# Block 0 enters w1's products centred only, and the tokens' scale is multiplied onto their sums

## The chip, the cores and the metric

The kernel runs on one core of one Trainium2 chip. The metric is the device time of one execution in microseconds (us), here the median of three timed runs. "Before" is the kernel as it stood, "after" the changed one.

## The reference

```python
xn = _layernorm(x, axis=-1)            # (x - mean) / sqrt(var + 1e-5), over 640 columns
A  = Real(DFT_seq(DFT_hidden(xn)))     # four einsums with the cosine and sine matrices
B  = gelu(xn @ w1 + b1) @ w2 + b2      # tanh gelu; w1 is 640 x 1536, w2 is 1536 x 640
out = x + A + B                        # x is 1 x 2048 x 640, fp32
```

What matters for the change: every token's row is centred by its mean and multiplied by one number of its own, 1/sqrt(var + eps). That number can be multiplied into the row before the product with w1, or onto the 1536 sums of that token after it, because it is the same for all 640 columns of a row.

## The kernel before, in words

The 2048 tokens are four blocks of 512, a block is four chunks of 128 rows. All products are in pairs of fp32r numbers: a value is split into a high part (a copy rounded by ScalarE, `high`, line 186) and a low part (what is left, subtracted by VectorE, `low`, line 189), and each product is three matmuls (high x high, high x low, low x high). So every operand that TensorE uses costs ScalarE one pass and VectorE one pass first.

The kernel's first stage, about 90 us long, is the MLP of block 0. It works in units of 128 of the 1536 hidden columns. `hidden(g)` (line 320) is 15 matmuls that accumulate w1's product of unit g in one of the PSUM banks 5, 6, 7; ScalarE takes gelu of the bank (line 340), the result is split, and `output(g)` (lines 300 to 302) is 15 matmuls into banks 0 to 4. The order on TensorE is hidden(0), hidden(1), hidden(2), output(0), hidden(3), output(1), and so on: in turn i of the loop at line 1157 come hidden(i+2) and output(i). Each turn also prepares W1[i+3] (`prep_w1`) and W2[i+1] (`prep_w2`), that is: a split of a weight piece that SyncE has loaded.

Beside that run pieces of other work, which `background(i)`, `late(i)` and `normalize_a` put into the turns: the statistics of the other blocks' rows (`ln_stats`, BN_STATS on VectorE), their scale (`ln_scale`, a square root on ScalarE and five small VectorE operations), the normalizing itself (`ln_apply`, line 231), and two rearrangements: the normalized rows of blocks 2 ("b") and 1 ("a") are moved within the on-chip memory into tiles z_b and z_a by 16 DMAs each (`put_z`, line 762; z_a lies in the tile `row`), and all rows are written to a DRAM tensor xn (`put_rows`, line 770). From z_b and z_a "forms" are made for the next stage: `make_forms` transposes a piece (line 259) and splits it. In before, forms of b are made in turn 4, those of a from turn 6 on.

All orders are written out by hand: each engine carries out its own list strictly in the order of the program, and waits at the first instruction whose inputs are not there. The same holds for SyncE's and GpSimd's lists of DMA issues.

The start. Four chunks of x are loaded; 19 matmuls on zeros (line 666) keep TensorE busy until then, and the first two weight loads wait for the first 7 and 10 of these (`NGATE`). The chunks' statistics are taken on VectorE (0, 2, 3: lines 215, 216) and on ScalarE (1: lines 692 to 699), the roots on ScalarE (690, 707) and polished by small VectorE operations (700 to 713), then the rows are normalized (714, 721 on ScalarE, line 236 on VectorE), 20 TensorE transposes turn them (line 682), and their results are split into XT (lines 186 and 189 under line 736). W1[0] is split at lines 723 and 734.

Of the kernel before, what the change touches and what calls it, by code (L numbers as in the profile page):

```python
# [10 lines left out]
F32 = mybir.dt.float32  # L11
F32R = mybir.dt.float32r
AF = mybir.ActivationFunctionType
# [6 lines left out]
NWARM = 19  # L20
# [6 lines left out]
def kernel(  # L27
# [105 lines left out]
    ident = early.tile([P, P], F32, name="ident")  # L133
    es_r = ExitStack()
# [41 lines left out]
    def split(hi, lo, src, perm=False):  # L176
# [6 lines left out]
        low(l, s, h)  # L183
# [26 lines left out]
    def ln_stats(c):  # L210
        m = MV
# [6 lines left out]
    def ln_scale(n):  # L218

        m = MV[:, :n]  # L220
        ve, r, t = m[:, :, 2], m[:, :, 3], m[:, :, 4]
# [7 lines left out]
    def ln_apply(c, eng=nc.vector):  # L229
        m = MV[:, slot[c]]  # L230
        eng.tensor_scalar(xt[c], xt[c], m[:, 0:1], m[:, 3:4], op0=ALU.subtract, op1=ALU.mult)

    def ln_apply_chunked(dst, c, j0=0, j1=ND):

        m = MV[:, slot[c]]
# [51 lines left out]
    def prep_w1(i, n=None):  # L287
        if i < NF:
            W1[i] = slots[1, i]
            split(W1[i][:, 0], W1[i][:, 1], w1r.pop(i if n is None else n).rearrange("p a b -> p (a b)"))  # L290

    def prep_w2(i):
        if i < NF:
            W2[i] = slots[2, i]
            split(W2[i][:, 0], W2[i][:, 1], w2r.pop(i), perm=True)
# [36 lines left out]
    def unit(g, acc, plus=None, a=None):  # L332
# [18 lines left out]
    FIRST = [(0, 0), (0, 2), (1, 0), (1, 2), (0, 1), (2, 0), (2, 2), (1, 1), (3, 0), (3, 2)]  # L351
    FIRST += [(2, 1), (4, 0), (4, 2), (3, 1), (4, 1)]
# [327 lines left out]
    def transpose_x(c, j0, j1):  # L680
# [5 lines left out]
    last = 1  # L686
    f, m = MV[:, 0], MV[:, last]
    root, step, shift = f[:, 3:4], f[:, 4:5], f[:, 5:6]
    ln_stats(0)
    nc.scalar.activation(root, f[:, 1:2], AF.Sqrt, bias=eps[:, 0:1])  # L690
    scratch = mr.tile([P, 2 * TB], F32, tag="hs", bufs=3, name="scratch")[:, :D]
    nc.scalar.activation(scratch, xt[last], AF.Copy, scale=-1.0 / D, accum_out=m[:, 5:6])
    nc.scalar.activation(
        chunked(xp[:, last]),
        xt[last].rearrange("p (q c i) -> p q c i", q=Q, i=B),
        AF.Identity,
        bias=m[:, 5:6],
    )
    nc.scalar.activation(scratch, xp[:, last], AF.Square, scale=D**-0.5, accum_out=m[:, 1:2])
    nc.vector.reciprocal(root, root)  # L700
    nc.vector.scalar_tensor_tensor(step, root, -0.5, root, op0=ALU.mult, op1=ALU.mult)
    nc.vector.scalar_tensor_tensor(step, f[:, 1:2], EPS, step, op0=ALU.add, op1=ALU.mult)
    for c in (2, 3):
        ln_stats(c)
    others = MV[:, 1:NC]
    v, r, t = others[:, :, 1], others[:, :, 3], others[:, :, 4]
    nc.scalar.activation(r, v, AF.Sqrt, bias=eps[:, 0:1])  # L707
    nc.vector.scalar_tensor_tensor(root, step, 1.5, root, op0=ALU.add, op1=ALU.mult)  # L708
    nc.vector.scalar_tensor_tensor(shift, f[:, 0:1], -1.0, root, op0=ALU.mult, op1=ALU.mult)
    nc.vector.reciprocal(r, r)  # L710
    nc.vector.scalar_tensor_tensor(t, r, -0.5, r, op0=ALU.mult, op1=ALU.mult)
    nc.vector.scalar_tensor_tensor(t, v, EPS, t, op0=ALU.add, op1=ALU.mult)
    nc.vector.scalar_tensor_tensor(r, t, 1.5, r, op0=ALU.add, op1=ALU.mult)
    nc.scalar.activation(  # L714
        chunked(xp[:, 0]),
        xt[0].rearrange("p (q c i) -> p q c i", q=Q, i=B),
        AF.Identity,
# [1039 lines left out]
```

## Time and profile before

| what | value |
|---|---|
| timed runs | 851.46, 851.7 and 852.76 us, median 851.7 |
| span of the profiled execution | 849.9 us, first to last instruction |
| what lies around the span | 1.8 us, taken as the median less the span; the profiled execution's own time is not listed apart |
| TensorE / weight loads / VectorE / ScalarE / GpSimd busy | 99% / 82% / 81% / 43% / 8% |
| granted TensorE clock, mean | 0.998 |
| DMA | 166.53 MB, 196 GB/s mean |

How to read what follows. "Idle before" an instruction is the time its engine had nothing to do, with what ended that time. The chain that ended last is followed back from the end of the kernel: whatever is not on it could have been longer without costing anything, up to its slack. A row with xN stands for N instructions in a row; its duration is from the start of the first to the end of the last, so the pitch of one is about a N-th of it.

### The profile page before, as it was taken

Reading aid. Unit: us, or ns where it says so; the run is one execution under the profiler, and the core shown is the slowest. Engines: PE = TensorE matmul, PEld = TensorE weight load, DVE = VectorE, ACT = ScalarE, POOL = GpSimd, SP = SyncE. Lnnn points to the kernel's source line nnn. Section 1 sums busy time; section 2 is a strip of 40 time slices with the busy share of each in tenths; the row PEclk is TensorE's granted clock in tenths of the full one; section 3 lists DMA queues with packets and bytes.
Section 4 is the critical chain, followed back from the end, with each engine's and each line's share of the span. In section 5 each row is a group of like instructions: output and inputs, shape, how many; then the busy total and the mean of one; then the engine's idle time right before and its main releaser. Section 6 shows DMA issues by size and latency. Waiting matters only on the chain.

```text
span 849.9 us, 10599 instructions
## 1 busy us (share of the span) xinstructions
PE 841.9 (99%) x3711; PEld 696.7 (82%) x3711; DVE 686.7 (81%) x909; ACT 368.6 (43%) x527; POOL 67.7 (8%) x116
## 2 busy tenths in 40 slices
PE   8999999999999999999999999999999999999997
PEld 7888888888888888888888888888888888888886
DVE  7979889767844778979978887889967998885687
ACT  7655666654453555443444344232323433323241
POOL 0440024222301000000000000000000000000002
PEclk9999999999999999999999999999999999999999
DMA  8995667878977897958744679763745799705464
GB/s 230 288 248 158 139 163 250 260 223 305 262 192 199 333 323 138 209 120 193 158 137 107 167 220 283 165 144 99 214 150 156 229 237 234 303 19 180 124 172 108
DMA packets 199141, 166.53 MB, mean 196 GB/s; under 512 B 61648, under 2 KB 170192, under 8 KB 198576
## 3 DMA queue, kind: packets, MB, share of 16 engines
q1 hardware_dynamic: 188320, 140.42, 62.7%
q0 software_dynamic: 7600, 24.91, 8.7%
q10 hardware_dynamic: 3168, 0.52, 0.3%
q8 instruction: 29, 0.48, 0.2%
q14 instruction: 24, 0.20, 0.1%
HBM read 115.75 MB, written 46.14 MB: 190 GB/s over the span
## 4 chain that ended last, share of the span: by engine, by line
PE 98%; DMA 1%; DVE 0%; ACT 0%; SPq 0%; issue 0%; ACTq 0%
PE banks L301 29%; PE banks L302 29%; PE banks L300 29%; PE banks L320 10%; DMA row<-in_A_x_dram 1%; PE banks L682 0%; DVE st L215 0%; ACT xp L714 0%; SPq L208 0%; DVE yo L1722 0%; DVE mv L216 0%; ACT mv L707 0%; DVE mv L708 0%; ACTq L707 0%
## 5 line engine op out<-in xcount | busy, mean ns | idle before, releaser
L186 ACT ACTIVATE as<-r 128x1024 fp32r<-128x1024 f32 x80 | 85.0, 1062 | 171.1 <-PE banks L302 150.4
L300 PE MATMUL banks<-as,xab 128*128 128x512 f32 x407 | 158.3, 389 | 0.0
L302 PE MATMUL banks<-as,xab 128*128 128x512 f32 x407 | 158.3, 389 | 0.0
L301 PE MATMUL banks<-as,xab 128*128 128x512 f32 x407 | 158.3, 389 | 0.0
L189 DVE TENSOR_TENSOR as<-r,as 128x1024 fp32r<-128x1024 f32 x80 | 97.2, 1215 | 38.1 <-ACT as L186 38.0
L301 PEld LDWEIGHTS banks<-as,xab 128*128 128x128 f32 x407 | 76.4, 188 | 15.9
L302 PEld LDWEIGHTS banks<-as,xab 128*128 128x128 f32 x407 | 76.4, 188 | 15.8
L300 PEld LDWEIGHTS banks<-as,xab 128*128 128x128 f32 x407 | 76.4, 188 | 15.8
L300 PE MATMUL banks<-as,xc 128*128 128x512 f32 x224 | 87.1, 389 | 0.0
L301 PE MATMUL banks<-as,xc 128*128 128x512 f32 x224 | 87.1, 389 | 0.0
L302 PE MATMUL banks<-as,xc 128*128 128x512 f32 x224 | 87.1, 389 | 0.0
L186 ACT ACTIVATE as<-rt 128x1024 fp32r<-128x1024 f32 x32 | 34.0, 1063 | 72.5 <-PE banks L302 57.9
L320 PE MATMUL banks<-xt,xab 128*128 128x512 f32 x240 | 56.8, 390 | 0.0
L189 DVE TENSOR_TENSOR hs<-ab,hs 128x512 fp32r<-128x512 f32 x36 | 24.7, 685 | 37.6 <-ACT hs L186 37.6
L320 PEld LDWEIGHTS banks<-xt,xab 128*128 128x128 f32 x240 | 45.0, 188 | 9.4
L301 PEld LDWEIGHTS banks<-as,xc 128*128 128x128 f32 x224 | 42.1, 188 | 8.8
L302 PEld LDWEIGHTS banks<-as,xc 128*128 128x128 f32 x224 | 42.0, 188 | 8.7
L300 PEld LDWEIGHTS banks<-as,xc 128*128 128x128 f32 x224 | 42.1, 188 | 8.7
L1280 POOL DMA_DIRECT2D out_dram<-u x4 | 2.6, 658 | 568.8 <-DVE u L463 568.8
L302 PE MATMUL banks<-hs,xc 128*128 128x512 f32 x120 | 46.7, 389 | 0.0
L300 PE MATMUL banks<-hs,xc 128*128 128x512 f32 x120 | 46.7, 389 | 0.0
L301 PE MATMUL banks<-hs,xc 128*128 128x512 f32 x120 | 46.7, 389 | 0.0
(240 smaller groups left out, 1678.9 us busy)
## 6 DMA issues: line engine op xcount, KB each, us to landing
raw<-in_A_dft_seq_re_dram SPq DMA_DIRECT2D x64, 256.0 KB, 5.4
raw<-in_A_dft_seq_im_dram SPq DMA_DIRECT2D x64, 256.0 KB, 5.1
w1r<-in_B_w_dram SPq DMA_DIRECT2D x144, 80.0 KB, 3.5
wit<-wst POOLq DMA_DIRECT2D x15, 384.0 KB, 4.2
wit<-wst POOLq DMA_DIRECT2D x20, 256.0 KB, 4.5
forms_ab<-xab SPq DMA_DIRECT2D x4, 1280.0 KB, 7.7
xab<-wit SPq DMA_DIRECT2D x13, 384.0 KB, 4.5
row<-xn SPq DMA_DIRECT2D x14, 320.0 KB, 5.3
```

The source lines that it names most:

```text
L186: nc.scalar.activation(h, s, AF.Copy)
L189: nc.vector.tensor_tensor(l, s, h.bitcast(F32), op=ALU.subtract)
L300: nc.tensor.matmul(acc, wh, mh, start=first, stop=False, skip_group_check=goes_on)
L301: nc.tensor.matmul(acc, wh, ml, start=False, stop=False, skip_group_check=goes_on)
L302: nc.tensor.matmul(acc, wl, mh, start=False, stop=last, skip_group_check=goes_on)
L320: nc.tensor.matmul(acc, W1[i][:, a, j * P : (j + 1) * P], XT[j][:, b], start=n == 0, stop=n == len(steps) - 1)
L1280: queues[q % len(queues)].dma_start(rows_of(out, t)[:, :, q * DQ + c0 : q * DQ + c1], src[q * B : (q + 1) * B])
```

## The change

- Chunks 0 to 3 are only centred before the transposes. Chunk 0 is centred by VectorE after its statistics, chunk 1 by ScalarE, chunk 2 by VectorE, chunk 3 by both; nothing waits for a root. The spread of chunk 3 and the four roots come after W1[1] is split.
- The scale (one number for each token) is turned by four TensorE transposes of a broadcast column, which stand after the first six matmuls of hidden(1), into bank 0; ScalarE copies it out. Each of the 12 units of block 0 gets a VectorE multiplication of its sums by this tile ahead of gelu.
- W1[0]'s high part moves from ScalarE to VectorE. 14 warm-up matmuls instead of 19.
- The normalizing of blocks 0 and 2 for z_b and xn moves from VectorE to ScalarE (`rows_beside`). Block 2's scale is made by a bit trick (two VectorE operations) and three Newton steps on GpSimd, 14 GpSimd operations in all with the shift; block 3's by the same steps on VectorE. Only block 1's scale keeps the square root of ScalarE.
- The low parts of W1[i+3] and W2[i+1] move behind the multiplication of unit i+2 on VectorE. From turn 4 on, the background comes after gelu(i+2).
- z_a's DMAs go out over GpSimd and SyncE in turn (before: GpSimd alone), xn's of block 2 over SyncE. Forms of a are made in turn 5 instead of 6, and so on.

```diff
-NWARM = 19
+NWARM = 14
...
+    def ln_scale(n, eng=nc.vector):
...
+        nc.vector.tensor_scalar(ve, m[:, :, 1], EPS, None, op0=ALU.add)
+        nc.vector.tensor_scalar(r.bitcast(I32), ve.bitcast(I32), -0.5, float(0x5F3759DF), op0=ALU.mult, op1=ALU.add)
+        for _ in range(3):
+            eng.tensor_tensor(t, r, r, op=ALU.mult)
+            eng.tensor_tensor(t, t, ve, op=ALU.mult)
+            eng.tensor_scalar(t, t, -0.5, 1.5, op0=ALU.mult, op1=ALU.add)
+            eng.tensor_tensor(r, r, t, op=ALU.mult)
...
+    def ln_apply_beside(c):
+        m = (MVA if 4 <= c < 8 else MV)[:, slot[c]]
+        nc.scalar.activation(xt[c], xt[c], AF.Identity, bias=m[:, 5:6], scale=m[:, 3:4])
...
+        if g < NF:
+            add(a, acc, scale, ALU.mult)
+            acc = a
         nc.scalar.activation(a, acc, AF.Gelu_apprx_tanh, bias=b1c[:, i : i + 1])
...
+    ln_stats(0)
+    centre(0)
+    mean_beside(1)
+    centre_beside(1)
+    spread_beside(1)
+    ln_stats(2)
+    centre(2, 0, 2)
+    mean_beside(3)
+    nc.vector.tensor_scalar(MV[:, 3, 0:1], MV[:, 3, 5:6], -1.0, None, op0=ALU.mult)
+    centre_beside(3, 0, 2)
+    centre(2, 2, ND)
+    centre(3, 2, ND)
     transpose_x(0, 0, ND)
+    transpose_x(1, 0, ND)
     transpose_x(2, 0, 2)
     transpose_x(3, 0, 2)
     transpose_x(2, 2, ND)
+    transpose_x(3, 2, ND)
+    W1[0], first_w1 = slots[1, 0], w1r.pop(0).rearrange("p a b -> p (a b)")
+    nc.vector.tensor_copy(W1[0][:, 0], first_w1)
     nc.vector.tensor_tensor(W1[0][:, 1], first_w1, W1[0][:, 0].bitcast(F32), op=ALU.subtract)
...
-    acc0 = hidden(0, slice(1, None))
+    acc0 = hidden(0)
     prep_w1(1)
-    acc1 = hidden(1)
+    spread_beside(3)
+    v, r, t = MV[:, :, 1], MV[:, :, 3], MV[:, :, 4]
+    nc.scalar.activation(r, v, AF.Sqrt, bias=eps[:, 0:1])
...
+    prep_w1(2)
     prep_w2(0)
-    prep_w1(2)
+    acc1 = hidden(1, slice(0, 6))
+    for c in range(NC):
+        nc.tensor.transpose(bank(0)[:, c * P : (c + 1) * P], MV[:, c, 3:4].to_broadcast([P, P]), ident)
+    hidden(1, slice(6, None))
+    scale = rows.tile([P, TB], F32, tag="yt", bufs=2, name="scale")
+    nc.scalar.activation(scale, bank(0), AF.Copy)
...
+    def rows_beside(i):
...
+        if i == 2:
+            Z["b"] = zo_tile("z_b")
+            for c in range(2 * NC, 3 * NC):
+                ln_apply_beside(c)
+            put_z(Z["b"], A["rows_b"], nc.gpsimd, nc.sync)
+            put_rows(2, A["rows_b"], nc.sync)
...
         if i == 1:
             ln_stats(11)
+            ln_scale(NC, nc.gpsimd)
+            ln_shift(nc.gpsimd)
...
-        if i == 6:
+        if i == 5:
             put_rows(1, A["rows_a"], nc.sync)
             new_forms(3, "t1")
             make_forms("a", "ua0", "ua1", "va0")
...
+        if i == 5:
+            add(ub, ub, ua, ALU.subtract)
...
-        put_z(Z["a"], A["rows_a"], nc.gpsimd)
+        put_z(Z["a"], A["rows_a"], nc.gpsimd, nc.sync)
...
     for i in range(NF - 2):
-        prep_w1(i + 3)
-        if i == 3:
-            normalize_a()
+        lows = []
+        prep_w1(i + 3, rest=lows)
...
-        prep_w2(i + 1)
+        prep_w2(i + 1, lows)
+        rows_beside(i)
+        if i < 4:
+            background(i)
+        acc = hidden(i + 2)
...
+        gelu(i + 2, acc, lambda k: [f() for f in lows] if k else None)
         if i + 6 < NF + 3:
             load_w1(i + 6)
         load_w2(i + 4)
-        background(i)
-        acc = hidden(i + 2)
...
-        gelu(i + 2, acc)
+        if i >= 4:
+            background(i)
         late(i)
         output(i)
```

In `gelu`, the function handed in as `fill` runs between the high and the low part of the unit, so `lows` (W1's and W2's low parts) stand on VectorE behind the unit's multiplication and ahead of its own low part. `late(3)` is now `normalize_a`. The loads of block 0's residual rows and of b2 move from turn 8 to turn 9.

More of the change, by code (lines that the diff above doesn't have):

```diff
@@ L182, in split @@
         high(h, s)
-        low(l, s, h)
+        if rest is None:
+            low(l, s, h)
+        else:
+            rest.append(lambda: low(l, s, h))
     def high(h, s):
@@ L699 @@
[L699 to L717, printed above, removed]
-        bias=shift,
-        scale=root,
-    )
@@ L1152, in fourier_step, with second @@
             form(2)
-    gelu(0, acc0)
-    gelu(1, acc1)
+    a0 = unit(0, acc0)
+    a1 = mr.tile([P, TB], F32, tag="ab", bufs=2, name="ab1")
+    def second(k):
+        if k:
+            add(a1, acc1, scale, ALU.mult)
+    split_unit(0, a0, second)
+    nc.scalar.activation(a1, a1, AF.Gelu_apprx_tanh, bias=b1c[:, 1:2])
+    split_unit(1, a1)
     for i in range(NF - 2):
-        prep_w1(i + 3)
-        if i == 3:
-            normalize_a()
+        lows = []
+        prep_w1(i + 3, rest=lows)
         if i == NF - 3:
```

120 lines of the change are left out of this document (65 added, 55 removed).

## The prediction

> **What bounds the kernel now.** First the page's busy times and its chain that ended last, then the same chain in order of time.
>
> ```profile
> PE 841.9 (99%) x3711; PEld 696.7 (82%) x3711; DVE 686.7 (81%) x909; ACT 368.6 (43%) x527; POOL 67.7 (8%) x116
> PE 98%; DMA 1%; DVE 0%; ACT 0%; SPq 0%; issue 0%; ACTq 0%
> 1.67 4.54 DMA row<-in_A_x_dram
> 6.23 0.90 DVE st L215 x2
> 7.36 0.76 DVE st L215 x2
> 8.66 0.91 ACT xp L714
> 9.71 2.27 PE banks L682 x19
> 25.79 3.40 PE banks L320 x15
> ```
>
> TensorE (PE) is the chain from 9.71 us to the end; ahead of it stand chunk 2's landing (1.67 + 4.54 = 6.21), the statistics and the normalizing. So a change can win only in the first 16 us, where TensorE waits for its operands, and it can lose wherever it makes TensorE wait later. A hidden(g) or an output(g) is 15 matmuls of 0.227, 3.40 us, and a turn 6.8.
>
> The second view is the timeline by engine, the start first.
>
> ```profile
> 0.75 1.82 SPq L208 DMA_DIRECT2D row<-in_A_x_dram  x4
> 1.44 1.10 DVE L657 CAST warm<-zeros 128x512 fp32r<-128x512 f32 x3
> 4.66 0.21 DVE L216 BATCH_NORM_AGGREGATE mv<-st 128x2 f32<-128x12 f32 x1
> 5.10 0.72 ACT L692 ACTIVATE scratch<-row 128x640 f32<-128x640 f32 x1
> 5.95 0.83 ACT L693 ACTIVATE xp<-row,mv 128x640 f32<-128x640 f32 x1
> 7.45 0.19 ACT L699 ACTIVATION_READ_ACCUMULATOR scratch<-xp 128x1 f32 x1
> 9.60 1.51 DVE L236 TENSOR_SCALAR xp<-row,mv 128x256 f32<-128x256 f32 x4
> 11.03 2.56 ACT L186 ACTIVATE xt<-banks 128x512 fp32r<-128x512 f32 x5
> 11.09 0.82 DVE L734 TENSOR_TENSOR xab<-w1r,xab 128x640 fp32r<-128x640 f32 x1
> 11.83 3.07 DVE L189 TENSOR_TENSOR xt<-banks,xt 128x512 fp32r<-128x512 f32 x5
> 22.23 0.39 PE L300 MATMUL banks<-hs,xc 128*128 128x512 f32 x1
> L666 PE MATMUL banks<-warm 128*128 128x512 f32 x12 | 5.4, 641 | 1.9 <-DVE warm L657 1.9
> DMA to landing us min/median/max: 3.0/4.0/4.9
> ```
>
> Output(0) starts at 22.23; hidden(1) and hidden(2) before it are 30 matmuls, so hidden(0) ended at 22.23 - 6.8 = 15.4. That is the mark to beat.
>
> **The start after the change.** x's four issues are some 0.46 apart from 0.75 on and land 3.0, 3.5 (twice the median less the third's), 4.54 (the chain's) and 4.9 later: 3.7, 4.7, 6.2, 7.0. ScalarE takes chunk 1 as in before (mean, centring, spread: from 5.10 to 7.64, 2.54 us), now from 4.7 on, to 7.2; then chunk 3's mean (0.9) to 8.1. VectorE negates it (some 0.2), centres the rest of chunks 2 and 3 (0.39 and 0.45 by the L236 row) to 9.1, copies W1[0] (1.10 / 3 for 512 columns, so 0.45 for 640) to 9.5, subtracts (0.74 to the next start) to 10.3, and takes five low parts of XT (0.60 each) to 13.3. The last matmul of hidden(0) waits for the fifth: hidden(0) ends at 13.65, **1.75 us sooner**. Were the copy as dear as the subtraction, it would be 1.4. TensorE hides none of this, and nothing else is late: 12 warm-up matmuls at 0.44 run to 7.2, two at 0.23 to 7.65, and the transposes follow the centred chunks to 9.8; ScalarE's five high parts (0.48 apart) run from 9.25 to 11.8.
>
> The four transposes of the scale cost TensorE 4 x 0.12 (2.27 / 19) = 0.48. Do they wait? Their place is six matmuls into hidden(1), at 15.0. The roots: ScalarE splits W1[1], takes chunk 3's spread and the root to 13.5; VectorE has W1[1]'s low part to 14.0 and four small operations (0.2 each) to 14.8. Cover 0.2; without it the transposes would wait by what is missing. So the start brings 1.75 - 0.48 = **-1.3** (between -0.9 and -1.8).
>
> **The turns.** Rows of the stage, those that set its waits:
>
> ```profile
> 1.06 0.29 POOL masks.py:199 TENSOR_SCALAR_AFFINE_SELECT ident<-ident 128x128 f32<-128x128 f32 x1
> 32.65 0.17 DVE L226 TENSOR_TENSOR mv<-mv 128x4 f32<-128x4 f32 x1
> 33.05 2.18 DVE L231 TENSOR_SCALAR r<-r,mv 128x640 f32<-128x640 f32 x4
> 33.91 0.74 ACT L186 ACTIVATE xab<-w1r 128x640 fp32r<-128x640 f32 x1 [1.72 <-DMA w1r<-in_B_w_dram]
> 35.90 4.36 POOL L762 DMA_DIRECT2D z_b<-r  x8 [8.54 <-ACT xc L186]
> 45.43 3.81 POOL L762 DMA_DIRECT2D row<-rt  x7 [2.76 <-DVE rt L231]
> 53.18 2.73 POOL L762 DMA_DIRECT2D row<-rt  x5 [1.13 <-DMA row<-rt]
> 58.38 0.69 DVE L189 TENSOR_TENSOR hs<-ab,hs 128x512 fp32r<-128x512 f32 x1 [0.42 <-ACT hs L186]
> 59.31 0.83 DVE L189 TENSOR_TENSOR as<-w1r,as 128x640 fp32r<-128x640 f32 x1 [0.24 <-ACT as L186]
> 62.69 1.30 DVE L259 STREAM_TRANSPOSE ztua<-row 128x512 f32<-128x512 f32 x2 [1.05 <-DMA row<-rt]
> 66.85 1.22 DVE L463 TENSOR_TENSOR z_b<-z_b,row 128x1024 f32<-128x1024 f32 x1
> 67.98 0.69 DVE L189 TENSOR_TENSOR hs<-ab,hs 128x512 fp32r<-128x512 f32 x1
> 66.43 2.88 PE L320 MATMUL banks<-xt,as 128*128 128x512 f32 x12
> 24.00:40.00 16.00, 16.00 (x72) 13.23 (x72) 14.99 (x38) 10.16 (x13) 6.43 (x12) 1.00 0.96 294
> 40.00:52.00 12.00, 12.00 (x55) 9.93 (x54) 9.69 (x22) 6.02 (x9) 8.39 (x16) 1.00 0.96 266
> 52.00:62.60 10.60, 10.60 (x49) 8.77 (x48) 6.64 (x10) 5.90 (x9) 2.78 (x6) 1.00 1.08 232
> ```
>
> The last three are stretches: width, their sum over cores, then PE, weight loads, VectorE, ScalarE, GpSimd busy, granted clock, DMA share, GB/s.
>
> *The multiplications.* Twelve of some 0.68 (a VectorE pass over a bank, as XT's) are 8.2 us more for VectorE; the normalizing of two blocks leaves it, 2 x 2.18. VectorE had 14.99 of 16 us busy from 24 to 40, so I walked its list. Hidden(1) ends at 13.65 + 3.4 + 0.48 = 17.5. Unit 0's and 1's multiplications end at 17.0 and 18.4, their low parts, behind ScalarE's gelu, at 19.6 and 20.9; two chunks' statistics (1.0 each) bring 22.9, unit 2's multiplication 23.6, W1[3]'s low part 24.3. Hidden(3)'s third matmul, the first that reads it, is due at 17.5 + 6.8 + 0.45 = 24.8: 0.5 to spare. So on: W2[1] 25.0, unit 2's low part 26.9 (behind ScalarE's four rows of block 0), two chunks 28.9, GpSimd's two forerunners 29.3, unit 3 30.0, W1[4] 30.75, due at 31.6. In turn 3 two chunks end at 42.0, block 1's root and its small operations at 43.1, unit 5 at 43.8, W1[6] at 44.6, due at 45.2. I take nothing, but cover is thin: each 0.1 us beyond it is 0.1 us on TensorE. A unit's own low part has more: unit 2's, at 26.9, is wanted by output(2) at 34.6. Two table loads fewer on ScalarE are off the path.
>
> *GpSimd's 14 operations.* Before has none of this kind. By the nearest rows: not below the 0.17 of VectorE's same operation; up to the 0.55 of a DMA issue, GpSimd's commonest instruction there (4.36 / 8). I take 0.29, the select's: 4.1 us from 29.3 on, to 33.4. ScalarE asks for it at 35.3, after W1[5] (landed at 33.9) and W2[3]. Beyond 0.43 each it delays z_b; at 0.55 by 1.7 us.
>
> *z_b.* ScalarE normalizes it from 35.3 in 4 x 0.65 to 38.0; its DMAs start at 38.1 (35.90 before). xn's four follow on SyncE, ahead of W1[8]'s load: that lands near 51 and is wanted at 55. Forms of b find z_b landed near 46 and are made from 51.4 (49.9 before, where they waited). No cost.
>
> *z_a and the forms of a.* Here I expect the loss. In before VectorE took W1[9]'s low part at 59.31, **ahead** of z_a's first transpose, which waited for DMA until 62.69. hidden(9) began at 66.43. That wait was free. In after the forms of a follow the unit's low part directly (ready at 58.4 by my walk, as at 58.38 + 0.69 before), and queued behind them in VectorE's list are their sum (L463), unit 8's multiplication and only then W1[9]'s low part. ScalarE's list has W1[9]'s high part behind the forms' too. If z_a lands at L, the forms and the sum take until L + 5.4 (62.69 to 67.98, with 0.1 for the start), the multiplication 0.6, the low part 0.8, the wake-up 0.1: L + 6.9. hidden(9) starts at 66.43 - 1.3 = 65.1 and needs it 0.45 later. TensorE waits **L - 58.7**.
>
> L is unknown. z_b is issued 2.2 us later than before; z_a's rows are normalized by 48.0 (unit 5's low part to 45.9, then 2.18), so its first issue comes at 48.7 (45.43 before, the last at some 55.9), half of it on SyncE behind xn's, W1[8], W2[6], W1[9] and W2[7]. The DMA engines were 0.96 to 1.08 busy from 24 to 62.6, so the bytes count: from z_b's first packet to z_a's last, 16 + 16 pieces of 80 KB, xn's 4 and W2's 2 of 320 KB, W1's 8 of 80 KB, 5.1 MB. At 294 GB/s that is 17.4 us, at 232 it is 22. Begun at 40 (2 us after the issue, since little is queued then): L between 57.4 and 62. A third way, before's own time from first issue to landing (35.9 to 62.6) set behind 38.1, gives 64.8, less some 2 for the queue that z_b no longer finds: 62.8. I take 61.5, near the slower rates, which are those of this very work. Wait 2.8; at the ends nothing and 6.1 (64.8).
>
> The Trainium skill's page "Trainium Kernel Development and Optimization", section "Key Constraints", speaks against the split over two queues: DMAs of SyncE, ScalarE and GpSimd run on the same 16 engines, and several issuers save issue time only. The DMA shares of 0.96 to 1.08 agree. By it the split does not shorten L.
>
> *The rest.* Block 3's scale on VectorE has nine more small operations (1.8 us, less a wait for ScalarE's root); they stand beside outputs whose operands are made a whole output (3.4 us) ahead. The residual's loads one turn later are wanted some 20 us on. Nothing.
>
> **The sum.** The profiled execution's 849.9 + 1.8 around it is the median of 851.7. 851.7 - 1.3 + 2.8 = **853.2**.
>
> **The rivals.** (a) *z_a is in time.* If L is 58.7 or less, which 294 GB/s would give, the start's gain stays whole: 851.7 - 1.3 = 850.4 (849.9 with the start's best). For it: from 24 to 40 the engines did move that much. Against: from 40 on, the time of this work, they did not. This is the other side, and it decides at L = 58.7.
>
> (b) *z_a is later, and TensorE stands long.* GpSimd at 0.55 each moves L to 63 and beyond; the wait is 4.5 to 6: 855 to 856.5. For: SyncE carries more than before ahead of its half of z_a. Against: GpSimd carries less. A stall of this length may also close the clock: at the start the first 12 warm-up matmuls, 5.4 us, had double pitch. That again would be 2.6 us more. TensorE's only wait in the trace, after the warm-up, is this one (us in total, times, longest):
>
> ```profile
> PE banks L682 <- ACT xp L714: 0.7, 1, 0.7
> ```
>
> The Trainium skill's page "TensorE: Matmul & The Clock Gate", part 1, has the clock halve after an idle window of about 3.4 us and open after a busy one. The 5.4 us of slow warm-up agree with the opening; no row here shows the closing.
>
> (c) *The start gives little*, since hidden(0) hangs on VectorE's list: with W1[0]'s copy dear and the scale's transposes late by 0.5, it is -0.4 and (the wait counted) 854.
>
> **How the numbers follow.** 0.55 for a wait of 1.5 to 4.5 us, (c) within it: 851.9 to 854.9. 0.27 for (a), 0.18 for (b). The range goes from 850.0 to 856.0. The bound of 0.2% is 1.7 us, about what a measurement here tells from no change. Slower than 853.4: (b) and half of the first, 0.45. Faster than 850.0: the best quarter of (a), 0.07. The same: 0.48.
>
> **What would show it.** Right: output(0) starts at about 20.9; the forms' first transpose of a waits for DMA past 60; hidden(9) starts two or more us behind output(6)'s end, its idle time put down to ScalarE or VectorE; no other TensorE gap over 0.3 us; GpSimd done before 35. Wrong: z_a landed before VectorE asks; a gap at hidden(3), (4) or (6), which would be the thin cover; z_b's issue after 40; a start above 21.3.

## The result, and the profile after

The changed kernel takes **861.0 us** (median of 4 runs, 860.1 to 862.0) against 851.6 for the kernel before (4 runs, 851.5 to 852.8): ratio 1.0104, 95% interval 1.0090 to 1.0119. Forecast were 853.2 us and a range up to 856. The profiled execution took 862.0; its span is 860.3 against the 849.9 of before, 10.3 us more before rounding.

Page of the profile, after: busy times, and the chain that ended last.

```profile
PE 846.2 (98%) x3710; PEld 697.1 (81%) x3710; DVE 690.5 (80%) x913; ACT 369.8 (43%) x530; POOL 65.6 (8%) x118
PE 87%; DMA 5%; DVE 2%; ACT 2%; SPq 1%; issue 1%; POOL 1%; DVEq 0%; ACTq 0%; POOLq 0%
```

TensorE was 98% of the chain; now 13% lies on other engines and DMAs, most of it in two stretches that are shown below. Its 846.2 us of busy time are 4.3 more, though the products are the same: part of them ran slower. Timeline, the start of after:

```profile
10.39 3.08 DVE L194 TENSOR_TENSOR xt<-banks,xt 128x512 fp32r<-128x512 f32 x5
15.26 0.60 PE L784 MATMUL banks<-ident,mv 128*128 128x128 f32 x4
21.16 0.39 PE L325 MATMUL banks<-hs,xc 128*128 128x512 f32 x1
```

Output(0) starts at 21.16, 1.07 us ahead of before's 22.23: the start gives what it should, nearly. Then GpSimd's scale for block 2, ScalarE's normalizing behind it, and z_b's first issues:

```profile
29.73 0.72 POOL L232 TENSOR_SCALAR mv<-mv 128x4 f32<-128x4 f32 x1
30.53 0.65 POOL L233 TENSOR_TENSOR mv<-mv 128x4 f32<-128x4 f32 x1
31.26 0.60 POOL L230 TENSOR_TENSOR mv<-mv 128x4 f32<-128x4 f32 x1
34.24 0.24 POOL L252 TENSOR_SCALAR mv<-mv 128x4 f32<-128x4 f32 x1
34.51 3.36 ACT L256 ACTIVATE r<-r,mv 128x640 f32<-128x640 f32 x4 [2.18 <-POOL mv L252]
38.18 2.23 POOL L796 DMA_DIRECT2D z_b<-r  x4 [3.70 <-ACT r L256]
```

SyncE's queue from there to z_a (start, time to issue, count): block 2's rows, W1[8], W1[9], and z_a's half only from 56.05 on. (W2[6] and W2[7], 0.4 us each, stand before and behind W1[9].)

```profile
44.17 3.71 SPq L804 DMA_DIRECT2D xn<-r  x4
47.99 4.35 SPq L303 DMA_DIRECT2D w1r<-in_B_w_dram  x4
52.94 1.98 SPq L303 DMA_DIRECT2D w1r<-in_B_w_dram  x4
56.05 6.24 SPq L796 DMA_DIRECT2D row<-rt  x8
```

VectorE's list behind it, with ScalarE's and TensorE's rows of the same place:

```profile
64.61 1.31 DVE L284 STREAM_TRANSPOSE ztua<-row 128x512 f32<-128x512 f32 x2 [3.07 <-DMA w1r<-in_B_w_dram]
69.90 0.68 DVE L491 TENSOR_TENSOR ab<-banks,scale 128x512 f32<-128x512 f32 x1
70.50 0.81 DVE L194 TENSOR_TENSOR as<-w1r,as 128x640 fp32r<-128x640 f32 x1
68.03 0.72 ACT L191 ACTIVATE as<-w1r 128x640 fp32r<-128x640 f32 x1
68.80 0.73 PE L345 MATMUL banks<-xt,as 128*128 128x512 f32 x2 [3.28 <-ACT as L191]
71.37 2.93 PE L345 MATMUL banks<-xt,as 128*128 128x512 f32 x6 [1.83 <-DVE as L194]
```

z_a's last piece lands at 63.8 and its first transpose starts at 64.61. (That row names a load of W1 as the releaser, but W1[9] had landed at 59.8; the chain below has z_a.) Behind it stand the forms of a, their sum, the multiplication of unit 8, and only then W1[9]'s low part; on ScalarE W1[9]'s high part stands behind the forms' too. Hidden(9) is due at 65.4 (66.43 less 1.06) and gets its first high part at 68.75 and its first low part at 71.3: TensorE waits 3.3 and 1.8 us by the rows, 5.6 with the steps between. The chain that ended last, in order of time, takes this very way:

```profile
52.45 6.01 DMA w2r<-in_B_w_dram
59.12 0.59 SPq L796
61.69 2.12 DMA row<-rt
64.61 0.72 DVE ztua L284
71.37 5.92 PE banks L345 x13
```

W2[6]'s landing lets SyncE go on, SyncE issues z_a piece by piece, the last piece lands, the forms follow, and TensorE. Between the landing and the first transpose the chain has 0.8 us of VectorE's sequencer, which takes the transpose's many waits one after the other: eight such rows (DVEq), 0.1 us from one to the next, here the first and the last.

```profile
63.84 0.05 DVEq L284
64.52 0.05 DVEq L284
```

z_a's 16 DMAs came over two queues. In e2 below, where GpSimd alone issues all 16, the chain has four such rows, and the transpose starts 0.4 us behind the last landing; in before it started 0.1 us behind it (62.57 and 62.69). So 0.4 to 0.7 us of TensorE's wait seem to come from the number of waits and not from the landing; no run tests this apart.

Stretches (width, their sum, PE, weight loads, VectorE, ScalarE, GpSimd busy with counts, **granted clock**, DMA share, GB/s):

```profile
64.00:66.00 2.00, 1.53 (x7) 0.94 (x5) 1.31 (x2) 0.64 (x2) 0.00 (x0) 1.00 0.71 159
66.00:72.00 6.00, 1.36 (x4) 0.83 (x5) 5.82 (x8) 3.82 (x6) 0.00 (x0) 0.90 0.88 280
72.00:78.00 6.00, 6.00 (x16) 4.73 (x15) 3.91 (x8) 2.48 (x5) 0.00 (x0) 0.53 0.70 201
```

From 72 to 78 TensorE is busy all the time, but with 16 matmuls where 6 us usually hold 28: the granted clock is halved, after the wait, for 6.8 us. Fifteen matmuls at 0.43 in place of 0.23 are 3.0 us.

The matmuls are the same and in the same order, so the start of the n-th one in both traces gives a **lag** behind before (worked out so, here and below). It is -1.06 from output(0) to 63 us, +7.5 behind hidden(9), +8.2 from 134 on, +9.4 from 272 to the last matmul (853.59 against 844.18), and 0.9 more lies behind that. So the whole: start -1.1, wait 5.6, clock 3.0, later 0.7 + 1.2 + 0.9 = 10.3. The 1.2 stand in the chain too:

```profile
218.47 11.15 DMA xab<-in_A_x_dram
232.48 5.15 DMA z<-row
239.94 5.63 DMA w1r<-in_B_w_dram
247.28 0.61 DVE hs L194
```

A load of x lands 11 us after its issue, block 3's z and a load of W1 come behind it, and a unit's low part behind that.

### The profile page after: what moved, and what is told of

Its sections match the earlier page's. It is cut to its first block, busy times and chain, and to the rows that moved or that the text cites. A ratio compares the mean times of both kernels' runs of the same rounds, so it can differ in the third digit from the quotient of the medians.

```text
span 860.3 us, 10620 instructions
## 1 busy us (share of the span) xinstructions
PE 846.2 (98%) x3710; PEld 697.1 (81%) x3710; DVE 690.5 (80%) x913; ACT 369.8 (43%) x530; POOL 65.6 (8%) x118
## 4 chain that ended last, share of the span: by engine, by line
PE 87%; DMA 5%; DVE 2%; ACT 2%; SPq 1%; issue 1%; POOL 1%; DVEq 0%; ACTq 0%; POOLq 0%
PE banks L325 27%; PE banks L326 27%; PE banks L327 27%; PE banks L345 7%; DMA xab<-in_A_x_dram 1%; DMA xab<-gs 1%; DMA w2r<-in_B_w_dram 1%; SPq L796 1%; DMA w1r<-in_B_w_dram 1%; DMA z<-row 1%; DMA row<-rt 1%; DMA row<-in_A_x_dram 1%; DVE st L220 0%; DVE xab L194 0%; ACT r L256 0%
## 5 line engine op out<-in xcount | busy, mean ns | idle before, releaser
L194 DVE TENSOR_TENSOR as<-r,as 128x1024 fp32r<-128x1024 f32 x80 | 97.2, 1216 | 38.1 <-ACT as L191 37.9
L345 PEld LDWEIGHTS banks<-xt,xab 128*128 128x128 f32 x240 | 44.8, 188 | 10.2 <-ACT xt L191 0.5
```

The costliest lines, as they stand in the source:

```text
L194: nc.vector.tensor_tensor(l, s, h.bitcast(F32), op=ALU.subtract)
L345: nc.tensor.matmul(acc, W1[i][:, a, j * P : (j + 1) * P], XT[j][:, b], start=n == 0, stop=n == len(steps) - 1)
```

## The experiments

Theory 1: the wait for z_a and what is queued behind it (with the clock) is the loss; 1b within it: the bytes ahead of z_a make it late, whatever its queue. Theory 2: VectorE's added load, the 12 multiplications, is the loss. In the course of the runs theory 2 was split: VectorE has no room (2a), or the multiplication ties other engines to VectorE's list (2b by its round trip, 2c by what stands ahead of it).

The lags are those at output(0), at the start of hidden(11), behind output(8) (80 us in before), behind the first pairs (114; a pair is a unit of the next stage's work, `pair(k)`) and at the last matmul. They belong to the one profiled execution of a run, the us to the median of its runs; the profile of e1 is its slowest run and that of e5 its fastest.

| run | us | ratio (95%) | lags |
|---|---|---|---|
| changed kernel | 861.0 | 1.009-1.012 | -1.1, +7.5, +7.5, +9.4 |
| e1_forms_later | 856.7 | 1.005-1.008 | -1.0, -0.2, +3.0, +5.2 |
| e2_za_gpsimd | 861.0 | 1.010-1.013 | -1.2, +9.2, +9.2, +9.8 |
| e3_xn_gpsimd | 858.9 | 1.007-1.010 | -0.9, +6.8, +6.8, +7.0 |
| e4_keep_busy | 860.3 | 1.009-1.012 | -1.1, +7.1, +7.2, +8.2 (15 idle matmuls not counted) |
| e5_later_no_mult | 854.6 | 1.002-1.005 | -1.2, -0.9, +0.5, +1.3 |
| e6_before_order | 862.2 | 1.011-1.014 | -0.9, +3.3, +8.6, +11.0 |
| e7_order_queues_root | 860.2 | 1.008-1.012 | -1.2, +2.0, +7.3, +7.5 |
| e8_start_only | 862.2 | 1.011-1.014 | -1.1, +4.8, +10.2, +10.2 |
| e9_dummy_mult | 861.9 | 1.011-1.014 | -0.9, +6.5, +11.8, +11.7 |
| e10_later_loads_root | 854.1 | 1.002-1.004 | -1.1, -1.1, +2.0, +2.1 |
| e11_loads_no_mult | 852.7 | 1.001-1.002 | -1.0, -0.2, +1.3, +1.3 |
| e12_xn_behind | 862.6 | 1.011-1.014 | -1.1, +9.5, +9.5, +11.9 |
| e13_dummy_apart | 851.7 | 0.999-1.001 | -1.1, -1.1, -0.7, -0.7 |
| e14_xn_other | 853.1 | 1.001-1.003 | -0.8, -0.8, -0.8, +0.7 |
| e15_bias_early | 854.8 | 1.002-1.005 | -1.2, -1.2, +1.7, +1.7 |
| e16_start_no_mult | 850.7 | 0.998-1.000 | -0.9, -0.9, -0.9, -0.9 |
| e17_za_ahead | 858.2 | 1.006-1.009 | -1.2, +3.6, +3.6, +5.9 |
| e18_za_quarter | 855.7 | 1.003-1.005 | -1.0, +3.6, +3.6, +3.7 |

### The order, the queue and the clock

**e1_forms_later**: the steps of the forms of a one turn later, as before the change.

```diff
-        if i == 5:
+        if i == 6:
             put_rows(1, A["rows_a"], nc.sync)
...
-        if i == 5:
-            add(ub, ub, ua, ALU.subtract)
...
+            add(ub, ub, ua, ALU.subtract)
+        if i == 7:
             make_forms("a", "oa0", "va1")
```

> After, with the forms of a (and what follows them) back one turn later, all else as in after; so VectorE takes unit 8's multiplication and W1[9]'s low part before it waits for z_a. Theory 1 (TensorE stands because these two are queued behind the wait for z_a's last transfer): the gap of 5.4 us ahead of hidden(9) and the half clock behind it (3.0 us) both go: 851 to 853, with z_a landing as late as before, near 64. Theory 2 (VectorE has too much to do since it multiplies every unit's sums; the wait is only where it shows): a gap of 2 us or more stays at a hidden unit from 9 to 11: 855 or more.

856.7 us. The wait at hidden(9) and the half clock are gone (the lag behind it is -0.2), but 5.2 us stay: by the lags 0.7 at hidden(8), 0.6 at hidden(11), 2.4 at the first pairs (two waits of 0.6 and 1.2 us by the rows), 0.5 near 130 and 1.6 between 204 and 250. The time lies in theory 2's range, without the gap of 2 us that it called for: theory 1 explains the stall and not the whole price.

**e2_za_gpsimd** (all of z_a on GpSimd's queue) and **e3_xn_gpsimd** (block 2's rows there):

```diff
-        put_z(Z["a"], A["rows_a"], nc.gpsimd, nc.sync)
+        put_z(Z["a"], A["rows_a"], nc.gpsimd)
```

```diff
-            put_rows(2, A["rows_b"], nc.sync)
+            put_rows(2, A["rows_b"])
```

> After, with z_a's 16 DMAs all issued by GpSimd, as in before. In after GpSimd's half landed by 56.7 and SyncE's half, queued behind block 2's rows and four weight loads, only at 63.8. Theory 1a (the order of issue on SyncE sets the landing): 16 issues of 0.55 from 48.2 on end at 57 and land by 61.5; the gap ahead of hidden(9) falls to about 2.7 us and the clock stays open: 854 to 856. Theory 1b (the DMA engines are full, so only the bytes count): landing near 64 as in after, 860 to 862.

> After, with block 2's rows for xn issued by GpSimd behind z_b, as in before, so that SyncE comes 3.7 us sooner to the weights and to its half of z_a. Theory 1a (order of issue on SyncE): z_a lands 2 to 3.5 us sooner, the gap falls to 2 to 3.5 us and the clock stays open: 854 to 857. Theory 1b (only the bytes count): 860 to 862.

z_a's first transposes start at 66.7 and 65.4 (64.6 in the changed kernel): neither queue helps z_a, as long as the same bytes go ahead of it. In e3 SyncE had 3.7 us of issues less, and yet it began z_a's half at 57.44, later than the 56.05 of the changed kernel: W1[8]'s four issues now took 6.1 us in place of 4.35. So 1a falls. e3's 858.9 lies between the two ranges; it is 2.2 us faster than the changed kernel, 0.7 of it at hidden(9) and the rest since the losses near 130 and from 204 on are nearly gone.

**e4_keep_busy**: 15 idle matmuls ahead of hidden(9).

```diff
+        if i == 7:
+            for _ in range(15):
+                nc.tensor.matmul(bank(6), W1[8][:, 0, :P], XT[0][:, 0], start=True, stop=True)
         acc = hidden(i + 2)
```

> After, with 15 more matmuls on TensorE ahead of hidden(9) whose sums nobody reads (3.4 us, into a bank that is free then). Theory 1 (the half clock comes from the idle time): the wait for z_a stays, since the 15 fit into it, but hidden(9)'s matmuls go at 0.227 instead of 0.427: 3 us less, 857.5 to 859. If the slow matmuls have another cause (their operands come late one by one), nothing changes: 860 to 862.

860.3, in the rival's range, but not for the rival's reason: the 15 fill the first part of the wait, the second, for W1[9]'s low part, stays, and the slow matmuls behind it go with a halved clock here too. Stretches of this run:

```profile
70.00:73.00 3.00, 1.17 (x5) 0.67 (x4) 3.00 (x5) 1.61 (x3) 0.00 (x0) 1.00 1.02 343
73.00:77.00 4.00, 4.00 (x12) 3.09 (x11) 3.11 (x5) 2.48 (x4) 0.00 (x0) 0.57 0.78 210
```

The clock still closes, for 3.4 us and not 6.8. So a wait of some 2 us can be enough to close it for 3.4 us; the longer one closed it for twice as long.

### What the multiplications cost

**e5_later_no_mult**: e1 without them.

```diff
-        if g < NF:
-            add(a, acc, scale, ALU.mult)
-            acc = a
```

> The same as the run with the forms one turn later, but the 12 multiplications of w1's sums by the tokens' scale are left out (the output then lacks the scale in the hidden layer). That run was 856.7 us, 5.2 us above the kernel before, with no wait left at hidden(9). Theory 2 (the 12 passes of some 0.68 us each make VectorE late, and its lateness shows at pair(0) and in the turns): most of the 5.2 us goes, 851 to 853 us, with TensorE's waits at the first pair gone. Its rival (the losses come from the order in which operands are made and loads are issued, not from VectorE's load): 855 to 857 us, with the waits at pair(0) still there.

854.6 us, 2.0 below e1; its profiled span of 852.0 has 1.2 us of TensorE waiting left, at the first pairs. Neither range is met: by the medians the multiplications cost 2.0 of e1's 5.2 us, by the lags, between e1's slowest and e5's fastest run, 3.9. So they cost something there, and how much stays unclear.

**e6_before_order** keeps the change's start and its queues but runs the turns from 4 on as before; **e7_order_queues_root** also puts block 2's rows on GpSimd's queue and takes block 3's scale from ScalarE's root; **e8_start_only** is the kernel before with nothing but the start and the multiplications.

```diff
-        if i < 4:
-            background(i)
+        background(i)
         acc = hidden(i + 2)
...
-        if i >= 4:
-            background(i)
```

```diff
-            put_rows(2, A["rows_b"], nc.sync)
+            put_rows(2, A["rows_b"])
...
-            ln_scale(NC)
+            ln_scale_table(NC, MV)
```

> The changed kernel with its start, its multiplications, GpSimd's scale and its two DMA queues, but from turn 4 on the turns run in the order of before: the background work ahead of the next hidden unit, W1's and W2's low parts not put off, the steps of the forms and the residual's loads in before's turns. Theory 1 (the loss is the order: what stands behind the wait for z_a in VectorE's list): no wait at hidden(9) over 0.5 us, 850.4 to 853 us. Theory 2 (VectorE's added load): waits spread over the turns and the first pair, 854 to 857 us.

> The run with the order of before, and block 2's rows on GpSimd's queue again, and block 3's scale from ScalarE's root as in before. Theory 1, with its side losses (xn's four issues on SyncE ahead of the weights, and VectorE's nine small operations at block 3): the late losses of about 1 us between 200 and 280 us go, so 850.4 to 852 us, about 1 us under the run with the order alone. If neither matters once nothing waits at hidden(9): the same as that run within 0.5 us.

> The kernel before with only the changed start: centred products for block 0, the 12 multiplications, the scale's four transposes, block 0's rows normalized by ScalarE. Block 2's scale stays on VectorE, z_a on GpSimd's queue, and the turns and the forms are those of before. Output(0) starts 1.06 us earlier in the changed kernel. Theory 1 (the multiplications cost nothing where no wait for z_a stands ahead of them): 850.4 us, 1.0 below before. Theory 2 (they make VectorE late): 853 us or more, with TensorE's waits between hidden(3) and the first pair.

862.2, 860.2 and 862.2: **as slow as the changed kernel, with none of its stall at hidden(9)**. Theory 1 said 850.4 to 853 for all three and falls as a full account: undo the order, and the price moves elsewhere. (In e7 the loss between 204 and 250, 1.7 in e6, is gone.) In e8 TensorE's 11 us are lost at hidden(6), (8), (11) and the first pairs. Timeline of e8 at hidden(11):

```profile
80.83 1.30 DVE L194 TENSOR_TENSOR xab<-ztt,xab 128x512 fp32r<-128x512 f32 x2
82.04 0.69 DVE L479 TENSOR_TENSOR ab<-banks,scale 128x512 f32<-128x512 f32 x1
82.76 0.72 ACT L356 ACTIVATE ab<-ab,b1c 128x512 f32<-128x512 f32 x1 [1.37 <-DVE ab L479]
84.05 0.72 ACT L191 ACTIVATE as<-w1r 128x640 fp32r<-128x640 f32 x1
84.83 4.10 PE L333 MATMUL banks<-xt,as 128*128 128x512 f32 x15 [1.93 <-ACT as L191]
```

and the same stretch of the kernel before:

```profile
77.03 0.67 ACT L340 ACTIVATE ab<-banks,b1c 128x512 f32<-128x512 f32 x1
80.03 2.20 PE L320 MATMUL banks<-xt,as 128*128 128x512 f32 x9
```

Read upwards from the last row of e8: TensorE waits for W1's high part on ScalarE; that stands behind the unit's gelu; the gelu waits for the multiplication; the multiplication stands in VectorE's list behind the forms, 2.5 us after its sums were ready (hidden(10) ended at 79.5). Before, the gelu read the bank and asked VectorE for nothing. Whether this is VectorE's load or the new tie took two steps to tell.

**e9_dummy_mult**: e8, gelu on the bank again, and a VectorE pass over bank and scale at each multiplication's place. **e13_dummy_apart**: the same, the pass reading only the scale's tile. **e16_start_no_mult**: e8 without any.

```diff
         if g < NF:
-            add(a, acc, scale, ALU.mult)
-            acc = a
+            add(scale, acc, scale, ALU.max)      # e9
+            add(scale, scale, scale, ALU.max)    # e13
```

> The run with the start only, which took 862.2 us, but the gelu of each of w1's 12 units reads TensorE's sums directly, as before the change, and the 12 multiplications are replaced by 12 VectorE passes of the same kind and size at the same places (bank and scale in, the larger of the two out to the scale's tile) whose result nothing reads; the output lacks the tokens' scale in the hidden layer. Theory 2a (the price is VectorE's 12 passes, 8.2 us of work): about as before, 860 us or more. Theory 2b (the price is the round trip: VectorE multiplies, ScalarE makes the gelu and the high part, and VectorE stands 1.45 us in front of the unit's low part with the rest of its list behind it): the waits in front of the low parts go from 16.4 us in all to about before's 5.4, and the time to 850 to 854 us.

> The run with the start only, 862.2 us, again with gelu reading TensorE's sums directly, and with 12 VectorE passes of the multiplications' size at their places, but these now read and write the scale's tile alone. In the run before with idle passes, which read the sums, ScalarE's gelu still waited for each of them (862 us); here nothing waits for a pass. The output lacks the tokens' scale in the hidden layer. Theory 2c (coupling: through the multiplication ScalarE's gelu, and W1's high part behind it, wait for all that stands ahead in VectorE's list; VectorE has room for the passes themselves): 850.4 to 853 us. Theory 2a (VectorE has no room for 8.2 us more): 858 us or more, with the same waits at hidden(6), (8) and the units behind.

> The run with the start only, 862.2 us, without the 12 multiplications (the output lacks the scale in the hidden layer). The start's gain by itself, 1.0 to 1.2 us at output(0): 850.4 to 850.8 us. If the other parts of the start (the rows of block 0 on ScalarE) cost something in the turns: above 852 us.

e9 took 861.9, and alone would have spoken for 2a. But its trace shows that the tie had not gone:

```profile
84.48 0.69 ACT L355 ACTIVATE ab<-banks,b1c 128x512 f32<-128x512 f32 x1 [1.37 <-DVE scale L478]
```

ScalarE still waited for a pass whose result it doesn't use; the two read the same bank. (Whether the bank or the order that the program is built with makes it wait isn't told apart here.) With the passes off the bank e13 takes **851.7 us**, 10.5 below e8 with the same VectorE work, and no wait of TensorE is left between 12 and 150 us. The same two groups of VectorE in e13 and, last, in e8 and in before (us busy, mean ns, us idle ahead of them and for whom), 16 to 115 us:

```profile
L194 DVE TENSOR_TENSOR hs<-ab,hs 128x512 fp32r<-128x512 f32 x15 | 10.3, 689 | 3.5 <-ACT hs L191 3.4
L478 DVE TENSOR_TENSOR scale<-scale 128x512 f32<-128x512 f32 x12 | 8.1, 674 | 0.1
```

```profile
L194 DVE TENSOR_TENSOR hs<-ab,hs 128x512 fp32r<-128x512 f32 x13 | 9.0, 692 | 16.4 <-ACT hs L191 16.4
L479 DVE TENSOR_TENSOR ab<-banks,scale 128x512 f32<-128x512 f32 x12 | 8.1, 672 | 0.7 <-PE banks L333 0.7
```

```profile
L189 DVE TENSOR_TENSOR hs<-ab,hs 128x512 fp32r<-128x512 f32 x15 | 10.2, 680 | 5.4 <-ACT hs L186 5.4
```

Twelve passes of 674 ns fit. What doesn't fit is that VectorE stands idle 16.4 us for the answer of a ScalarE that it kept waiting itself. 2a falls: as mere work the twelve cost at most the 1.0 us between the medians of e13 and e16 (0.1 by the lags), of the 11 that e8 loses. The tie between the two engines is the cause. 2b and 2c are its two directions, both go with it in e13, and no run tells them apart. e16 gives the start alone: 850.7, a lag of -0.9 that is kept to the end.

### How much is left when the order suits the multiplication

**e10_later_loads_root** is e1 with the residual's and the bias's loads in turn 8, block 2's rows on GpSimd and ScalarE's root for block 3; **e11_loads_no_mult** the same without multiplications; **e15_bias_early** is e10 with the bias's loads in turn 5.

```diff
-        if i == 9:
+        if i == 8:
             load_xo(0)
```

```diff
+        if i == 5:
+            for q in range(Q):
+                nc.sync.dma_start(b2c[...], b2[...])
         if i == 4:
             open_place(*PLACES[7])
```

> The run with the forms one turn later (856.7 us) and, beside it, the residual's and the output bias's loads in turn 8 as before the change, block 2's rows on GpSimd's queue, and block 3's scale from ScalarE's root as before. If the waits of that run at the first pair (2.4 us, where ScalarE waits for the bias's DMA) and between 200 and 250 us (1.5 us) come from these three: 852.5 to 853.5 us. If they come from VectorE's multiplications: still 855 to 857 us.

> The run with later forms, loads in turn 8, block 2's rows on GpSimd's queue and ScalarE's root for block 3, without the 12 multiplications (the output lacks the scale in the hidden layer). With no wait left, the start's gain alone stays: 850.4 to 851 us. If the run with the multiplications beside it is within 0.7 us of it, the multiplications cost nothing there.

> The run with later forms, loads in turn 8 and ScalarE's root (854.1 us), with the output bias's four small loads in turn 5 in place of turn 8. In that run ScalarE waits 0.8 us for them at 98.5 and TensorE's two waits of 0.6 and 1.4 us at the first pairs follow. If they come from it: 852 to 852.8 us. If VectorE's list makes them: 854 us.

e10 854.1, e11 852.7, so with the multiplication ahead of the forms (background work behind the gelu) the twelve cost 0.8 us by the lags and 1.4 by the medians, against the 0.7 that the expectation set as none. e11 itself misses its range: without any multiplication 0.8 is lost at hidden(8) and 1.5 at the first pairs, so this order of the forms has a price of its own. e10 is 2.5 below e1, about half of e1's 5.2: by the lags 0.7 at hidden(8), 0.4 near 130 and all of the 1.6 between 204 and 250 are gone, and the first pairs still lose 2.2 of 2.4. Which of its three edits does which isn't told apart here. e15's 854.8 is no gain: ScalarE's wait for the bias goes, and TensorE's wait at the first pairs is then put down to VectorE:

```profile
PE banks L325 <- DVE zc L491: 1.5, 1, 1.5
PE banks L345 <- DVE as L194: 0.3, 1, 0.3
```

So the bias was only the one of two operands, late together, that came last.

### Why z_a was late

**e12_xn_behind**: the changed kernel, block 2's rows stored behind z_a (and block 3's root). **e14_xn_other**: block 1's rows stored twice in turn 5 instead, so that no tile is held.

```diff
-            put_rows(2, A["rows_b"], nc.sync)
...
             normalize_a()
+            put_rows(2, A["rows_b"], nc.sync)      # e12
...
             put_rows(1, A["rows_a"], nc.sync)
+            put_rows(2, A["rows_a"], nc.sync)      # e14, in turn 5
```

> The changed kernel (861.0 us) with the four 320 KB writes of block 2's rows moved behind z_a's half on SyncE's queue, and block 3's scale from ScalarE's root. The order of the forms stays one step sooner. If the bytes in front of z_a set its landing: 1.3 MB less, at 232 to 294 GB/s 4.4 to 5.6 us sooner, so z_a's first transposes start near 59.5 and not at 64.6, TensorE's wait in front of hidden(9) falls to about 1, its clock stays open, and the time is 852 to 854 us. If the issue order or VectorE's list sets it: 859 us or more.

> The changed kernel, but block 2's rows are not stored from their own tile ahead of W1[8]; in their place block 1's rows are stored a second time, behind block 1's own in turn 5, so the same bytes follow z_a and no tile is held for them (the stored rows of block 2 are wrong). If the 1.3 MB in front of z_a on SyncE's queue made it late: z_a lands near 59 and not at 63.8, TensorE's wait for it falls from 5.7 to about 1 us and the clock stays open, 853 to 857 us. If not: 859 us or more with z_a at 63 to 64.

In e12 z_a lands at 58.9, 4.9 us sooner, as the bytes said, and the run is slower still (862.6). Its VectorE:

```profile
66.05 0.82 DVE L194 TENSOR_TENSOR r<-w2r,r 128x640 fp32r<-128x640 f32 x1 [9.01 <-ACT r L191]
67.93 1.30 DVE L284 STREAM_TRANSPOSE ztua<-row 128x512 f32<-128x512 f32 x2
```

W2 is split into the tile that the moved stores still read (they land at 64.8), and VectorE stands 9 us for it. So e12 says when z_a lands and nothing of the time. e14 holds no tile: 853.1 us, no wait of TensorE between 12 and 150 us, the clock open, and the lists of VectorE, ScalarE and TensorE are the changed kernel's.

```profile
51.04 5.65 SPq L796 DMA_DIRECT2D row<-rt  x8
59.18 1.31 DVE L284 STREAM_TRANSPOSE ztua<-row 128x512 f32<-128x512 f32 x2 [0.45 <-DMA w1r<-in_B_w_dram]
```

The bytes ahead of z_a are what e12 and e14 took away, and in both it landed 5 us sooner. So 7.9 us of the changed kernel's 861.0 hang on when z_a lands; the sum, the multiplication and W1[9] behind it in VectorE's list cost nothing once it is in time.

**e17_za_ahead**, complete: z_a's SyncE half issued ahead of W1[9] and W2[7], and block 3's root. **e18_za_quarter**: also three quarters of z_a on GpSimd.

```diff
+        if i == 3:
+            late(i)
         if i + 6 < NF + 3:
             load_w1(i + 6)
...
-        put_z(Z["a"], A["rows_a"], nc.gpsimd, nc.sync)
+        put_z(Z["a"], A["rows_a"], nc.gpsimd, nc.gpsimd, nc.gpsimd, nc.sync)      # e18 alone
```

> The changed kernel (861.0 us), complete, with z_a's half on SyncE's queue issued ahead of W1[9]'s and W2[7]'s loads (0.64 MB) in place of behind them, and block 3's scale from ScalarE's root. If z_a's landing sets the stall: at 232 to 294 GB/s it lands 2.2 to 2.8 us sooner, 61 to 61.6, the wait falls from 5.7 to 2.3 to 2.9 us, the clock stays open, the late 1 us goes: 852.5 to 854 us. If something else on the queues holds z_a: 858 us or more.

> The run with z_a's SyncE half ahead of W1[9], but with only a quarter of z_a (4 of 16 issues) on SyncE and three quarters on GpSimd, so that SyncE, held by W1[8]'s slow issues until 52, has 2.5 us of them and not 5.1. If the issue on SyncE ends z_a: it lands near 59 to 60, a wait of 0 to 1.3 us, 850.7 to 852.5 us, the fastest version of the change. If the bytes alone end it: as the run beside it, 852.5 to 854 us.

858.2 and 855.7. z_a lands at 60.9 and 61.2, so the place on the queue is worth 2.9 us of landing and the other split nothing: 1b, the bytes ahead of z_a, stands. Both miss their ranges. The transposes start at 61.9 and 62.0, the waits are some 3 us, and the clock closes for 3.4 us, which the expectations had open:

```profile
61.94 1.31 DVE L284 STREAM_TRANSPOSE ztua<-row 128x512 f32<-128x512 f32 x2
68.71 3.53 PE L345 MATMUL banks<-xt,as 128*128 128x512 f32 x10 [1.83 <-DVE as L194]
70.00:74.00 4.00, 4.00 (x12) 3.14 (x11) 3.02 (x6) 2.48 (x4) 0.00 (x0) 0.57 0.89 276
```

None of the kernels that do all the work beats the kernel before: the best is e10, 2.5 us above it.

## Why the prediction was wrong, point by point

- **The bound and the start: right.** TensorE's wait at hidden(9) is the place that was named, and the start gave -1.06 of the -1.3: VectorE stood 0.23 us for W1[0]'s load, the XT low parts and the transposes took 0.1 longer each. e16 shows the gain by itself (-0.9), kept to the end.
- **The multiplications at nothing: right in this order only.** The lag stays -1.06 to 63 us, so the thin covers of 0.5 to 0.9 us held. That the order decides was not seen: the prediction asked whether VectorE's list has room for the passes, and not what ScalarE's gelu loses that now waits for this list. With the forms ahead of it the multiplication costs 11 us (e8 against e16).
- **GpSimd: right.** 0.29 each to 33.4 forecast; 0.20 to 0.24 with three of 0.60 to 0.72, to 34.5, measured. z_b's issue at 38.1 was met to 0.2.
- **W1[8] "lands near 51": wrong by 6 us.** It landed at 56.9, behind xn's four (3.7 us to issue) and its own slow issues (4.35). Hidden(8) came through with nothing to spare; in e1 0.7 us were lost there.
- **z_a's landing L: the step that failed.** "The bytes count" gave L between 57.4 and 62, a third way gave 64.8, and "I take 61.5" took 2 us off for a queue thought empty. The last piece landed at 63.8. The 5.1 MB were counted well (5.3 MB went over from 38.0 to 63.8), but at 206 GB/s and not at 232 to 294: SyncE began its half only at 56.05, its eight issues took 6.2 us, and from 60 to 63.8 the DMA engines were 0.58 busy and moved 137 GB/s. Then came 0.8 us, not "0.1 for the start", before the first transpose. By that start less 0.1, the prediction's L was 64.5.
- **The wait: right as a rule, wrong in size.** The rule, a wait of L - 58.7, is borne out: 5.8 by it and 5.6 measured here, 3.1 and about 3.1 in e17, 0.4 and nothing in e14. So the mechanism held, and the term of 2.8 in the sum was 5.6. By the same rule the start's gain drops out of the sum as soon as TensorE waits, since hidden(9) cannot start sooner than its operand: rival (c)'s 854 keeps the wait at 2.8 though a start 0.9 worse makes it 0.9 shorter, and should have been 853.2 as well.
- **The clock: left out of the sum.** It stood in rival (b) alone, as a possibility worth 2.6; it cost 3.0. The rival's time, 855 to 856.5 plus 2.6, is 2 us from the result, and neither its chance (0.18) nor the range took the clock in.
- **"The rest. Nothing": wrong by 2.8 us.** 0.7 near 130, 1.2 between 204 and 272, 0.9 behind the last matmul. The middle one follows a load of the residual's x whose last piece is 11.2 us under way (9.8 in before). Block 3's scale isn't its cause, since e12 and e17 take ScalarE's root and lose 1.7 and 1.6 there; e2, e3, e7, e10 and e18 lose nothing. The record sorts the runs another way: all eight that lose 0.4 to 1.7 us there (the changed kernel, e1, e4, e5, e6, e12, e14, e17) have GpSimd issue half of z_a and none of block 2's rows, and in the eleven that lose nothing GpSimd issues at least four of these DMAs more. Why that would act 150 us later is not shown, and the other two losses stay open.
- **The miss as a whole.** 853.2 was forecast, and the profiled execution, at 862.0 one us above the median, missed it by 8.8: 2.8 for z_a's wait, 3.0 for the clock, 2.8 for the rest and 0.2 for the start.

## What to carry to other kernels

Where an operation moves onto an engine with a long list, ask not only whether the list has room for it but who must now wait for everything ahead of it in that list: twelve passes cost 1 us at most as work for VectorE, and 11 us as a link between VectorE and ScalarE. When work is called for sooner, ask when its operand lands and what stands ahead of it there: taking 1.3 MB from ahead of z_a brought it 5 us sooner, 0.64 MB 2.9 us, and the same bytes on another queue nothing. Look at what lies between the landing and the first use, too (0.8 us here), and price the clock with the wait: 2 us of waiting can cost 1.5 us more.

## What the runs showed of the hardware

- The clock halves for 3.41 us or twice that, and a stretch that is half busy can close it. In the 3.41 us ahead of its closing TensorE was busy 0.73 us in the changed kernel, 1.58 in e17 and 1.84 in e6. Of the stretches of this length, counted off from the clock's changes, that did not close it, the least busy have 1.60 (63.9 to 67.3 in the changed kernel), 1.69 (e6), 1.88 (e2) and 1.90 (e7, e8). So in these runs up to 1.58 always closed it, 1.88 and more never did, and between them it went both ways. The Trainium skill's page "TensorE: Matmul & The Clock Gate", part 1, has the clock closed by an idle window of about 3.4 us that runs freely; the length agrees, but here windows with 1.58 and 1.84 us of work closed it, so the measured rows decide.
- GpSimd's operations of 4 columns take 0.20 us, but the three from 29.73 to 31.86 took 0.60 to 0.72, and they end with VectorE's three low parts, which read two tiles of SBUF and end at 30.4, 31.1 and 31.8. The Trainium skill's page "SBUF — State Buffer", section "SBUF: two separate sides", has such a VectorE pass hold a port that GpSimd shares for its whole length; the trace agrees.
- VectorE's sequencer takes 0.1 us for each of the rows in which it passes a transpose's waits: eight rows, 0.78 us, in the changed kernel and e4, where z_a comes over two queues, and four, 0.37 us, in e2, where it comes over one. Where the last landing is met by the last row (before), only 0.1 us of it shows.
